# Attention in pairs of tiles: grouping TensorE's whole-array and 64x64 matmuls, with two PSUM tiles for the transposed rows

## The chip, the core and the metric

The kernel runs on one core of a Trainium2 chip. Its time is the device time of one launch in microseconds (us). Before the change the median of three runs is 567.77 us (565.73 to 568.13).

## The reference

An attention over chunks of 64 positions feeds a mixture of experts that picks one expert for each row.

```python
# attention: q, k, v are (8, 8, 576, 64); 9 chunks of 64 for each batch and head
scores = (1 / sqrt(64)) * q_c @ k_c.T            # 64 x 64 for each chunk
attn = exp(scores - max(scores)); attn /= sum(attn) + 1e-9
x = (attn @ v_c), heads side by side             # 4608 rows of 512
# mixture of experts: 8 experts, 512 -> 1024 -> 512
logits = x @ w_gate + modality_bias[modality_id]
e = argmax(logits); gate = softmax(logits)[e]
out = gate * (relu(x @ w1[e]) @ w2[e])
```

## The kernel before

**Attention.** The 4608 rows are 36 tiles of 128 rows (two chunks of 64, all 8 heads). The loop at line 731 takes one tile i at a time, in program order on every engine. For a tile t there are these steps, which run in different turns of the loop:

- scores(t), line 232: TensorE multiplies q by k in 16 pieces of 64x64 into the PSUM tile sp (L239). VectorE takes the row maximum (mx, L241) and subtracts it (ex, L243).
- exps(t), line 246: ScalarE takes exp in place (ex, L248); GpSimd folds the 64 columns to 32 (sr, L249). sums(t), line 251: VectorE sums sr (sm, L253) and takes the reciprocal (ris, L254).
- transposes(t), line 256: four 128x128 transposes of ex on TensorE (ap, L260); ScalarE copies them to SBUF (at, L262).
- values(t), line 265: 16 products of 64x64 with v (xp, L273); ScalarE copies them (xt, L276).
- rows(t), line 279: four whole-array matmuls turn xt back to rows and give the logits (yb, L288). VectorE scales the rows into xr (L290), ScalarE copies the logits (lp, L294) and then issues the write of xr to DRAM (xd, L295).

In turn i TensorE does transposes(i), rows(i-2), scores(i+2) and values(i). The transposes and the rows use the whole array of 128x128; the scores and values work in quarters of 64x64. An fp32 matmul of the program shows as two in the trace, so a step of 16 shows as x32, the rows as x8 and the transposes as x4. [...]

**Loads.** SyncE issues the loads of q and k (load_qk, L113, six buffers) and of v (load_v, L119, five buffers), each when its buffer comes free.

**Routing.** route(g), line 300, works on the logits of a group of tiles. Group 0 has tiles 0 to 13; its steps are the yields of a generator, and advance() takes one more of them after values of each tile (before values it advances only the scatters, as long as fewer than four of those have been issued). In this order the steps are: a product on GpSimd (L309), sums on GpSimd (L314 to L317), the maximum and exp (gmx, L321; ge on ScalarE, L324), one-hot and a prefix sum (oh, scan, L333 and L341), the rest of the prefix sum and a reciprocal, and then two TensorE matmuls (rp, L352 and L353) whose result gives each row its place in a table (pi, L362). 14 scatters by GpSimd (tab, L372) write that table, one for each advance().

**From the table to the first expert.** A table PLAN, by tile number counted from the end of attention, says after which tile SyncE fetches weights (raw, L588) and the row lists (tl, L510), GpSimd gathers the first expert's rows (xg, L531), and ScalarE and VectorE split weights into high and low parts (wh, L599; wl, L603). In the last two turns split(0) and split(1), line 565, transpose the gathered rows (tp, L571) in place of scores; split(2) and split(3) follow. Then come 13 slots of expert work (first, L628, and second, L642), which use yb's three banks as accumulators.

Of the kernel before, what the change touches and what calls it, by code (L numbers as in the profile page):

```python
# [8 lines left out]
F32 = mybir.dt.float32  # L9
# [10 lines left out]
P = 128  # L20
N = B * S
DM = H * D
E = 8
# [68 lines left out]
def attention_moe(ctx: ExitStack, tc: tile.TileContext, qkv, mod, cst, bias, wcat, wfst, out):  # L92
# [17 lines left out]
    def load_qk(t):  # L110
        if t < NT:
            b = wk.tile([P, 2, DM], F32, name="qk", bufs=NB)
            SP.dma_start(b, qkv[t][:, 0:2])  # L113
            st[t] = {"qk": b}
# [46 lines left out]

    yb = ps.tile([P, 3, 512], F32, name="yb", bufs=1)

    def busy(n):
        wps = ps.tile([P, 512], F32, tag="r", name="wps", bufs=1)
        for i in range(n):
            PE.matmul(wps, warm[:, 0:P], warm, start=True, stop=True)

# [110 lines left out]
    def rows(t):  # L279
# [5 lines left out]
        xr = wk.tile([P, NJB, NK, 32], F32, name="xr", bufs=4)  # L285
        fp = yb[:, 0:2, :].rearrange("p b (a c) -> p (b a) c", a=2)
        for p in range(NP):
# [6 lines left out]
        A.copy(lp.rearrange("p (a b) d -> p a (b d)", a=NP), fp[:, :, P:GWC])  # L294
        A.dma_start(xd[t * P:(t + 1) * P, :], xr.rearrange("p j c d -> p (j c d)"))  # L295

# [3 lines left out]
    def route(g):  # L300
# [48 lines left out]
        for _ in range(1 if g < NEG else 5):  # L349
            yield  # L350
        rp = ps.tile([P, 2, 32, E], F32, tag="r", name="rp", bufs=1)
        PE.matmul(rp[:, 0, 0:n], ub, oh, start=True, stop=True)  # L352
# [309 lines left out]
    def slot(s, mid=None):  # L662

        nt = tiles(s)
        end = max(s + 1, NSURE) * NF
        ys = [yb[:, t, :] for t in range(nt)]
        pend = None
# [60 lines left out]
    scores(1)  # L728
    load_qk(NB + 1)
    busy(BUSY)  # L730
    for i in range(NT):
        transposes(i)
        if i + 1 < NT:
            exps(i + 1)
        sums(i)
        load_v(i + NB - 2)
        if i >= 2:
            rows(i - 2)
        if i + 2 < NT:
            scores(i + 2)  # L740
        else:
            split(i + 2 - NT, "s")
        load_qk(i + NB + 2)
        if i >= 6 and i % 3 == 0:
            clear_part()
        advance([pooljobs] if len(marks) < 4 else None)
        values(i)
        advance()
        for g, (a, n) in enumerate(GROUPS):
            if a + n - 1 == i - 2:  # L750
                jobs.append(route(g))
        plan(i - NT)
    rows(NT - 2)
    split(2)
    split(3)
    plan(0)

    def last():
        rows(NT - 1)
        jobs.append(route(len(GROUPS) - 1))  # L760

# [74 lines left out]
```

## Time and profile before

| | |
|---|---|
| median of 3 runs (range) | 567.77 us (565.73 to 568.13) |
| the profiled execution | 568.66 us |
| its span, first to last instruction | 566.8 us |
| its mean granted TensorE clock | 0.996 |
| busy: TensorE, VectorE, ScalarE, GpSimd | 552.4, 362.3, 246.8, 179.7 us |
| chain that ended last: TensorE | 77% |
| attention, from the first transposes to the first expert matmul | 9.6 to 140.2 us |

The span is 1.9 us shorter than the execution's own time, which in turn is 0.9 us above the median of the runs. In rows of the timeline the columns are the start in us, the length in us, the engine, the line, the operation, its output and inputs, the number of instructions merged into the row and, in brackets, how long the engine had been idle before it and what ended that. PE is TensorE's matmuls, DVE is VectorE, ACT ScalarE, POOL GpSimd; a q behind a name is that engine's instruction queue.

### The profile page before, as it was taken

Reading aid. Unit: us, or ns where it says so; the run is one execution under the profiler, and the core shown is the slowest. Engines: PE = TensorE matmul, PEld = TensorE weight load, DVE = VectorE, ACT = ScalarE, POOL = GpSimd, SP = SyncE. Lnnn points to the kernel's source line nnn. Section 1 sums busy time; section 2 is a strip of 40 time slices with the busy share of each in tenths; the row PEclk is TensorE's granted clock in tenths of the full one; section 3 lists DMA queues with packets and bytes.
Section 4 is the critical chain, followed back from the end, with each engine's and each line's share of the span. In section 5 each row is a group of like instructions: output and inputs, shape, how many; then the busy total and the mean of one; then the engine's idle time right before and its main releaser. Section 6 shows DMA issues by size and latency. Waiting matters only on the chain.

```text
span 566.8 us, 12365 instructions
## 1 busy us (share of the span) xinstructions
PE 552.4 (97%) x4900; PEld 499.2 (88%) x4900; DVE 362.3 (64%) x633; ACT 246.8 (44%) x423; POOL 179.7 (32%) x182
## 2 busy tenths in 40 slices
PE   8999999999999999999999999999999999999993
PEld 5899999998889989899898998998898989989992
DVE  4777789867899665655656565565646656556741
ACT  3555555555434344443533434344434343344530
POOL 3312336732658753133230412213041220302101
PEclk9999999999999999999999999999999999999998
DMA  8999998968888647876574866657587673747400
GB/s 305 400 355 371 358 284 288 292 223 333 243 262 239 235 133 253 324 243 211 168 280 144 272 242 181 245 170 256 185 261 245 173 252 112 234 175 242 165 23 26
DMA packets 59538, 133.23 MB, mean 235 GB/s; under 512 B 11022, under 2 KB 29134, under 8 KB 53072
## 3 DMA queue, kind: packets, MB, share of 16 engines
q1 hardware_dynamic: 46784, 101.39, 54.0%
q0 software_dynamic: 7072, 19.18, 10.0%
q10 hardware_dynamic: 5616, 11.80, 5.5%
q8 instruction: 40, 0.66, 0.4%
q14 instruction: 26, 0.21, 0.1%
HBM read 102.16 MB, written 30.70 MB: 234 GB/s over the span
## 4 chain that ended last, share of the span: by engine, by line
PE 77%; issue 13%; POOL 3%; DMA 2%; DVE 2%; ACT 1%; SPq 0%; POOLq 0%; ACTq 0%
PE yb L642 29%; PE hp L628 28%; PE sp L239 6%; PE yb L288 6%; PE xp L273 6%; PE ap L260 3%; POOL out L657 1%; DMA out<-yo,tk 1%; DMA qk<-in_qkv 1%; POOL xg L531 1%; POOL lh L314 0%; DVE wl L603 0%; DVE xr L290 0%; ACT wh L599 0%; POOL lh L315 0%
## 5 line engine op out<-in xcount | busy, mean ns | idle before, releaser
L603 DVE TENSOR_TENSOR wl<-raw,wh 128x1024 fp32r<-128x1024 f32 (+1 forms) x106 | 129.3, 1221 | 35.0 <-ACT wh L599 35.0
L632 ACT ACTIVATE hh<-hp 128x384 fp32r<-128x384 f32 (+1 forms) x104 | 49.3, 474 | 200.6 <-PE hp L628 197.9
L628 PE MATMUL hp<-xl,wh 128*128 128x384 f32 (+1 forms) x416 | 136.4, 328 | 0.1
L628 PE MATMUL hp<-xh,wh 128*128 128x384 f32 (+1 forms) x416 | 136.4, 328 | 0.0
L628 PE MATMUL hp<-xh,wl 128*128 128x384 f32 (+1 forms) x416 | 136.2, 327 | 0.0
L633 DVE SCALAR_TENSOR_TENSOR hl<-hp,hh 128x384 fp32r<-128x384 f32 (+1 forms) x104 | 55.6, 535 | 103.2 <-ACT hh L632 103.2
L642 PE MATMUL yb<-wh,hl 128*128 128x512 f32 x296 | 117.3, 396 | 0.5 <-DVE hl L633 0.5
L642 PE MATMUL yb<-wh,hh 128*128 128x512 f32 x296 | 117.4, 397 | 0.0
L642 PE MATMUL yb<-wl,hh 128*128 128x512 f32 x296 | 116.7, 394 | 0.0
L657 POOL DMA_INDIRECT out<-yo,tk x37 | 47.2, 1275 | 215.8 <-DVE yo L656 187.6
L599 ACT CAST wh<-raw 128x1024 fp32r<-128x1024 f32 (+1 forms) x106 | 108.6, 1025 | 0.2 <-issue 0.2
L628 PEld LDWEIGHTS hp<-xl,wh 128*128 128x128 f32 x416 | 78.2, 188 | 4.2 <-DVE xl L573 0.4
L628 PEld LDWEIGHTS hp<-xh,wh 128*128 128x128 f32 x416 | 78.3, 188 | 4.1 <-ACT xh L572 0.3
L628 PEld LDWEIGHTS hp<-xh,wl 128*128 128x128 f32 x416 | 78.4, 188 | 0.0
L642 PEld LDWEIGHTS yb<-wh,hl 128*128 128x128 f32 x296 | 55.9, 189 | 14.9 <-DVE hl L633 1.4
L642 PEld LDWEIGHTS yb<-wl,hh 128*128 128x128 f32 x296 | 55.7, 188 | 9.6
L642 PEld LDWEIGHTS yb<-wh,hh 128*128 128x128 f32 x296 | 55.6, 188 | 9.0
L531 POOL DMA_INDIRECT xg<-xd,tk x37 | 44.7, 1208 | 21.6 <-issue 12.5
L249 POOL TENSOR_TENSOR sr<-ex 128x256 f32<-128x256 f32 x36 | 26.1, 726 | 68.4 <-ACT ex L248 68.2
L372 POOL DMA_INDIRECT tab<-tg,pi x36 | 39.3, 1092 | 16.7 <-issue 9.4
L239 PEld LDWEIGHTS sp<-qk 64*64 64x64 f32 x1152 | 36.9, 136 | 7.8 <-DMA qk<-in_qkv 2.4
L239 PE MATMUL sp<-qk 64*64 64x64 f32 x1152 | 41.9, 222 | 1.8 <-DMA qk<-in_qkv 1.5
(128 smaller groups left out, 534.2 us busy)
## 6 DMA issues: line engine op xcount, KB each, us to landing
raw<-in_wcat SPq DMA_DIRECT2D x48, 1024.0 KB, 5.8
qk<-in_qkv SPq DMA_DIRECT2D x36, 512.0 KB, 5.3
v<-in_qkv SPq DMA_DIRECT2D x36, 256.0 KB, 6.4
xd<-xr ACTq DMA_DIRECT2D x36, 256.0 KB, 5.8
xs<-xg SPq DMA_DIRECT2D x10, 768.0 KB, 5.7
xq<-xs SPq DMA_DIRECT2D x40, 192.0 KB, 3.5
tab<-raw ACTq DMA_DIRECT2D x3, 768.0 KB, 6.8
raw<-in_wfst SPq DMA_DIRECT2D x4, 512.0 KB, 7.8
```

Of the source, the lines that this page charges most:

```text
L239: PE.matmul(sp[cs_, h, :], b[cs_, 0, hs], b[cs_, 1, hs], start=True, stop=True)
L273: PE.matmul(xp[hs, p, c * 64:c * 64 + 64], v[hs, vs], at[hs, p, c * 64:c * 64 + 64], start=True, stop=True)
L288: PE.matmul(fp[:, p, 0:GWC], xt[:, p, :], gw[:, p, :], start=True, stop=True)
L372: w = G.indirect_dma_start(tab, bass.IndirectOffsetOnAxis(ap=pi[:, j:j + 1], axis=0), tg[:, j, :], None, bounds_check=E * CAP - 1, oob_is_ ...
L531: G.indirect_dma_start(xg[:, t, :], None, xd[0:n, :], bass.IndirectOffsetOnAxis(ap=tk[:, t:t + 1], axis=0), bounds_check=n - 1, oob_is_err ...
L599: A.copy(hi, raw)
L603: (G if pool else V).tensor_tensor(lo, raw, hi.bitcast(F32), ALU.subtract)
L628: PE.matmul(hp, a[:, ks], b[:, k, 0:n], start=(m == 0), stop=(m == 3 * NK - 1))
L632: A.activation(hh[:, 0:n], hp, AF.Relu)
L633: V.scalar_tensor_tensor(hl[:, 0:n], hp, 0.0, hh.bitcast(F32)[:, 0:n], ALU.max, ALU.subtract)
L642: PE.matmul(y, a[:, tsl], b[:, DM:2 * DM], start=(f == 0 and i == 0), stop=(f == NF - 1 and i == 2))
L657: w = G.indirect_dma_start(out, bass.IndirectOffsetOnAxis(ap=tk[:, t:t + 1], axis=0), yo, None, bounds_check=N - 1, oob_is_err=False)
```

## The change

The loop takes two tiles, i and i+1, in one turn. TensorE now does rows(i-2), transposes(i), rows(i-1), transposes(i+1), then scores(i+2), scores(i+3), values(i), values(i+1). In the first turn scores(2) and scores(3) follow the transposes of tile 0 and of tile 1.

- yb becomes two PSUM tiles of two banks each; rows of even tiles use the first, rows of odd tiles the second. The tag "r" is gone: busy writes into the second yb tile, and rp shares the tag "t" with ap and xp. The experts' three accumulators are both banks of the first tile and one of the second.
- The write of xr to DRAM leaves rows() and becomes put(), two of them in ScalarE's queue behind both tiles' copies.
- exps(t+2) stands behind values(t) now, where it stood ahead of scores(t+1); sums(i+1) stands at the end of the turn.
- The loads keep their order by tile; SyncE now gets one v, two qk and one v in each turn.
- The jobs still go forward by one step after values of each tile, and PLAN is still worked off by tile number. split(0) and split(1) both stand ahead of the last two values, with TensorE's transposes of tiles 34 and 35 just before them.

```diff
-    yb = ps.tile([P, 3, 512], F32, name="yb", bufs=1)
+    yb = [ps.tile([P, 2, 512], F32, name=f"yb{i}", bufs=1) for i in range(2)]
 
     def busy(n):
-        wps = ps.tile([P, 512], F32, tag="r", name="wps", bufs=1)
         for i in range(n):
-            PE.matmul(wps, warm[:, 0:P], warm, start=True, stop=True)
+            PE.matmul(yb[1][:, 1], warm[:, 0:P], warm, start=True, stop=True)
...
-        fp = yb[:, 0:2, :].rearrange("p b (a c) -> p (b a) c", a=2)
+        fp = yb[t % 2].rearrange("p b (a c) -> p (b a) c", a=2)
...
-        A.dma_start(xd[t * P:(t + 1) * P, :], xr.rearrange("p j c d -> p (j c d)"))
+        st[t] = xr
+
+    def put(t):
+        A.dma_start(xd[t * P:(t + 1) * P, :], st.pop(t).rearrange("p j c d -> p (j c d)"))
...
-        rp = ps.tile([P, 2, 32, E], F32, tag="r", name="rp", bufs=1)
+        rp = ps.tile([P, 2, 32, E], F32, tag="t", name="rp")
...
-        ys = [yb[:, t, :] for t in range(nt)]
+        ys = [yb[t // 2][:, t % 2] for t in range(nt)]
...
+    exps(1)
     busy(BUSY)
-    for i in range(NT):
-        transposes(i)
-        if i + 1 < NT:
-            exps(i + 1)
+
+    for i in range(0, NT, 2):
+        for t in (i, i + 1):
+            if i:
+                rows(t - 2)
+            transposes(t)
+            if not i:
+                scores(t + 2)
+        load_v(i + NB - 2)
+        if i:
+            put(i - 2)
+            put(i - 1)
         sums(i)
-        load_v(i + NB - 2)
-        if i >= 2:
-            rows(i - 2)
-        if i + 2 < NT:
+        if 0 < i < NT - 2:
             scores(i + 2)
-        else:
-            split(i + 2 - NT, "s")
+            scores(i + 3)
+        elif i:
+            split(0, "s")
+            split(1, "s")
         load_qk(i + NB + 2)
-        if i >= 6 and i % 3 == 0:
+        load_qk(i + NB + 3)
+        if any(t >= 6 and t % 3 == 0 for t in (i, i + 1)):
             clear_part()
         advance([pooljobs] if len(marks) < 4 else None)
-        values(i)
-        advance()
+        for t in (i, i + 1):
+            values(t)
+            if i < NT - 2:
+                exps(t + 2)
+            advance()
+            if t == i:
+                load_v(i + NB - 1)
+                plan(i - NT)
+                advance([pooljobs] if len(marks) < 4 else None)
+        sums(i + 1)
         for g, (a, n) in enumerate(GROUPS):
-            if a + n - 1 == i - 2:
+            if i and a + n - 1 == i - 1:
                 jobs.append(route(g))
-        plan(i - NT)
+        plan(i + 1 - NT)
     rows(NT - 2)
+    put(NT - 2)
```

What this moves can be seen in the engines' instruction lists. TensorE, two tiles in the middle of attention, before (the number behind a name tells buffers apart; x16 are the program's matmuls of one step):

```order
L239 MATMUL sp_1404<-qk_1033 64x64 x16
L273 MATMUL xp_1427<-at_1387,v_1131 64x64 x16
L260 MATMUL ap_1455<-cs_73,ex_1353 128x128 x4
L288 MATMUL yb_103<-cs_73,xt_1374 128x144 x4
L239 MATMUL sp_1477<-qk_1098 64x64 x16
L273 MATMUL xp_1500<-at_1460,v_1195 64x64 x16
L260 MATMUL ap_1524<-cs_73,ex_1423 128x128 x4
L288 MATMUL yb_103<-cs_73,xt_1444 128x144 x4
```

and two tiles now:

```order
L238 MATMUL sp_898<-qk_554 64x64 x16
L238 MATMUL sp_919<-qk_556 64x64 x16
L272 MATMUL xp_944<-at_875,v_633 64x64 x16
L272 MATMUL xp_967<-at_889,v_708 64x64 x16
L287 MATMUL yb0_103<-cs_73,xt_961 128x144 x4
L259 MATMUL ap_998<-cs_73,ex_917 128x128 x4
L287 MATMUL yb1_104<-cs_73,xt_984 128x144 x4
L259 MATMUL ap_1012<-cs_73,ex_938 128x128 x4
```

The steps of 64x64 of both tiles stand together, and so do the whole-array ones: two changes between the kinds in a pair where there were four. Rows of the second tile go to a tile of their own (yb1).

VectorE, from the last steps of group 0's prefix sum (scan) to the first instruction that reads rp (base1), before:

```order
L341 TENSOR_TENSOR scan1_137<-scan0_136 128x112
L341 TENSOR_TENSOR scan0_136<-scan1_137 128x112
L345 TENSOR_REDUCE gs_1590<-ge_1449 128x14
L346 TENSOR_SCALAR gs_1590<-gs_1590 128x14
L348 RECIPROCAL tg0_140<-gs_1590 128x14
L253 TENSOR_REDUCE sm_1603<-sr0_149 128x8
L254 RECIPROCAL ris_148<-sm_1603 128x8
L290 TENSOR_TENSOR xr_1608<-yb_103,ris_148 128x4x4x32
L241 TENSOR_REDUCE mx_1633<-sp_1616 128x8
L243 TENSOR_TENSOR ex_1635<-sp_1616,mx_1633 128x512
L354 TENSOR_TENSOR base1_133<-base0_132,rp_1658 128x8
```

and now, from the scores of the pair on:

```order
L240 TENSOR_REDUCE mx_1577<-sp_1560 128x8
L242 TENSOR_TENSOR ex_1579<-sp_1560,mx_1577 128x512
L240 TENSOR_REDUCE mx_1598<-sp_1581 128x8
L242 TENSOR_TENSOR ex_1600<-sp_1581,mx_1598 128x512
L343 TENSOR_TENSOR scan1_137<-scan0_136 128x112
L343 TENSOR_TENSOR scan0_136<-scan1_137 128x112
L347 TENSOR_REDUCE gs_1629<-ge_1488 128x14
L348 TENSOR_SCALAR gs_1629<-gs_1629 128x14
L350 RECIPROCAL tg0_140<-gs_1629 128x14
L356 TENSOR_TENSOR base1_133<-base0_132,rp_1656 128x8
```

The work of a whole tile that lay between scan and rp is gone from there: both now lie in one pair, behind the scores of both its tiles. On TensorE rp still stands behind the values of tile 21.

GpSimd around the gather of the first expert's rows (tk, xg), before:

```order
L249 TENSOR_TENSOR sr0_149<-ex_2190 128x8x32
L249 TENSOR_TENSOR sr1_150<-ex_2286 128x8x32
L527 COPY tk0_173<-tl0_172 128x3
L531 DMA xg_178<-xd_69,tk0_173 128x512 x3
L249 TENSOR_TENSOR sr2_151<-ex_2350 128x8x32
```

and now:

```order
L248 TENSOR_TENSOR sr0_149<-ex_2204 128x8x32
L248 TENSOR_TENSOR sr1_150<-ex_2225 128x8x32
L248 TENSOR_TENSOR sr2_151<-ex_2364 128x8x32
L529 COPY tk0_173<-tl0_172 128x3
L533 DMA xg_178<-xd_69,tk0_173 128x512 x3
L248 TENSOR_TENSOR sr0_149<-ex_2385 128x8x32
```

sr2 of tile 32 stands ahead of the gather now; the first sum behind the gather is that of tile 33.

More of the change, by code (lines that the diff above doesn't have):

```diff
@@ L759, in last @@
         rows(NT - 1)
+        put(NT - 1)
         jobs.append(route(len(GROUPS) - 1))
```

## The prediction

> **What bounds the kernel now.** I read the busy times by stage first, then the timeline of one tile, then the rows of single lines, and last the waits near the end of attention. Attention and the experts:
>
> ```profile
> 9.60:140.20 130.60, 128.41 (x2678) 120.10 (x2677) 101.38 (x235) 70.55 (x148) 49.21 (x62) 1.00 0.93 325
> ```
>
> The columns are the stretch, its length, the busy time of TensorE, its weight loads, VectorE, ScalarE and GpSimd, the granted clock, the DMA engines' busy share and GB/s. TensorE is busy for 128.4 of attention's 130.6 us. But busy is not full: one tile in the middle shows it.
>
> ```profile
> 72.21 1.03 PE L273 MATMUL xp<-at,v 64*64 64x64 f32 x29
> ...
> 74.80 1.15 PE L239 MATMUL sp<-qk 64*64 64x64 f32 x32
> 75.78 1.10 PE L273 MATMUL xp<-at,v 64*64 64x64 f32 x32
> 76.82 0.65 PE L260 MATMUL ap<-cs,ex 128*128 128x128 f32 x4
> 77.31 1.15 PE L288 MATMUL yb<-cs,xt 128*128 128x144 f32 x8
> 78.38 1.15 PE L239 MATMUL sp<-qk 64*64 64x64 f32 x32
> ```
>
> ```profile
> 69.82 0.49 PE L260 MATMUL ap<-cs,ex 128*128 128x128 f32 x3
> ```
>
> ```profile
> L273 PE MATMUL xp<-at,v x1152: 218/218/267, 11.1 to 138.5; 64*64 64x64 f32 x192
> ```
>
> A tile lasts 78.38 - 74.80 = 3.58 us, and no row in it shows an idle time ahead of it. Now the same matmuls at their own pace. The 29 values last 1.03 us from the first start to the last end; without the last one's 0.218 that is 28 steps in 0.81, 0.029 each, so the 64 of a tile take 1.85. Three transposes last 0.49, one is 0.273 (its median in the line's row), so a step is 0.11 and four take 0.44. The eight rows last 1.15, one is 0.286, a step is 0.123 and eight take 0.98. Together 3.27 us. The remaining 0.31 lies where the kind of matmul changes, twice in a tile: about 0.15 from values to transposes and 0.15 from rows to scores. Rounding in the rows makes it 0.29 to 0.31; I take 0.30. So attention is bound by TensorE's order, and 8% of a tile is the changes.
>
> **The change part by part.** *Changes of kind.* After the first transposes there are now 36 blocks of 64x64 work, one for each tile; with pairs there are 19 (scores(2) alone, then 17 pairs, then the last two values). 17 blocks fewer, each with a way in and a way out: 17 x 0.30 = **5.1 us less**. A pair should take 2 x 3.27 + 0.30 = 6.84 us.
>
> [...]
>
> [...]
>
> *Is a pair still bound by TensorE?* Count from the first scores matmul of a pair: scores to 1.85, values to 3.7, a change, rows at 3.85, transposes at 4.83, rows at 5.27, transposes at 6.25, next scores at 6.84. ScalarE and VectorE in one tile before:
>
> ```profile
> 72.42 0.69 DVE L241 TENSOR_REDUCE mx<-sp 128x8 f32<-128x512 f32 x1 [0.34 <-PE sp L239]
> 73.14 0.69 DVE L243 TENSOR_TENSOR ex<-sp,mx 128x512 f32<-128x512 f32 x1
> ...
> 73.35 0.58 ACT L276 COPY xt<-xp 128x512 f32<-128x512 f32 x1 [1.03 <-PE xp L273]
> ...
> 73.75 0.42 DVE L253 TENSOR_REDUCE sm<-sr 128x8 f32<-128x264 f32 x1
> ...
> 74.20 0.20 DVE L254 RECIPROCAL ris<-sm 128x8 f32<-128x8 f32 x1
> 74.46 0.63 ACT L248 ACTIVATE ex<-ex 128x512 f32<-128x512 f32 x1
> ...
> 74.97 0.69 DVE L290 TENSOR_TENSOR xr<-yb,ris 128x512 f32<-128x512 f32 x1 [0.56 <-DMA v<-in_qkv]
> ```
>
> The scores of this tile start at 74.80 - 3.58 = 71.22; mx follows 1.2 us later, and xt 1.14 us after the values' second matmul (72.21). So the first tile's xt is copied from 3.0 to 3.6, and its rows want it at 3.85: 0.25 to spare, the thinnest cover in the pair. exp of the next tile follows to 4.2 (wanted by the transposes at 4.83), then the second xt to 4.8 (wanted at 5.27) and the second exp to 5.45 (wanted at 6.25). VectorE: 2.69 us a tile, 5.4 of 6.84. Its chain mx, ex, mx, ex runs from 1.2 to 4.0. So a regular pair has no new wait. The two yb tiles let the rows of the second tile run without the evacuation of the first.
>
> *Loads and writes.* Loads of the same bytes come in another grouping; SyncE waits for TensorE to free buffers, not the reverse:
>
> ```profile
> SPq L113 <- PE sp L239: 41.2, 21, 2.3
> ```
>
> ```profile
> xd<-xr ACTq DMA_DIRECT2D x36, 256.0 KB, 5.8
> ```
>
> A q, k load is wanted three pairs, about 20 us, after its issue, and a v load two pairs. The two writes, moved behind both tiles' copies in ScalarE's queue, take 0.33 us each to issue, between 1.1 and 1.8 of the pair, before xt at 3.0. I cost these edits at nothing; if that cover fails, it is rival C.
>
> *Routing.* Two of its steps now wait for a whole pair's scores. The first:
>
> ```profile
> 84.49 0.46 DVE L341 TENSOR_TENSOR scan<-scan 128x112 bf16<-128x112 bf16 x2
> ...
> 87.56 0.22 PE L352 MATMUL rp<-oh,ub 128*128 128x112 bf16 x1
> ```
>
> Before, rp came 2.6 us after the scans and waited for nothing. Now the scans follow the second ex, which starts at 1.2 + 0.72 + 0.62 + 0.72 = 3.26; 0.61 later they start, 0.46 later they end, at 4.35, perhaps 0.3 more because the pair before gives VectorE two steps too. TensorE reaches rp at 3.85. Behind rp stand the rows of the pair and everything after: **0.6 us more**, once (0.3 to 1.0).
>
> ```profile
> 77.93 0.30 ACT L324 ACTIVATE ge<-lg 128x112 f32<-128x112 f32 x1 [0.42 <-DVE lg L322]
> ...
> 113.37 0.62 ACT L599 CAST wh<-raw 128x512 fp32r<-128x512 f32 x1
> ```
>
> The others are on ScalarE. ge, which needs the same late place on VectorE, now stands before a second xt: xt ends near 5.4, wanted at 5.27. The first wh cast (0.62 us) stands before a second xt too, and two xh casts of split before the xt of the last tiles. About 0.15 each, **0.4 us more** (0 to 0.8).
>
> *The gather.* Before, it cost TensorE a wait:
>
> ```profile
> 111.93 0.99 POOL L372 DMA_INDIRECT tab<-tg,pi  x1 [0.16 <-issue]
> ...
> 119.36 3.20 SPq L510 DMA_DIRECT2D tl<-tab  x3
> ...
> 126.11 1.00 POOL L531 DMA_INDIRECT xg<-xd,tk  x1 [0.30 <-issue]
> 127.13 1.41 POOL L249 TENSOR_TENSOR sr<-ex 128x256 f32<-128x256 f32 x2
> 127.59 0.66 PE L260 MATMUL ap<-cs,ex 128*128 128x128 f32 x4
> 127.90 0.43 DVE L253 TENSOR_REDUCE sm<-sr 128x8 f32<-128x264 f32 x1 [3.29 <-POOL sr L249]
> ...
> 129.46 1.25 PE L288 MATMUL yb<-cs,xt 128*128 128x144 f32 x8 [1.22 <-ACT lp L294]
> ```
>
> sr queued behind the gather, sm behind sr, xr and lp behind sm, and the rows behind lp: they start at 129.46 where 127.59 + 0.49 = 128.08 was due, 1.4 us late. Now sr of tile 32 is ahead of the gather, and sr of tile 33, behind it, is read only at the end of the next pair. Its sums run out at about 3.4 of that pair, and sm wants it at 4.0. **1.2 us less** (0 to 1.4).
>
> Sum: -5.1 + 0.6 + 0.4 - 1.2 = -5.3 us. The profiled execution (568.66, span 566.8) would become 563.4 (561.5); it is 0.9 above the median of the runs, so the median goes to 567.77 - 5.3 = **562.5 us**. The experts' order is not changed, and their stage shifts as a whole if its first inputs come in time.
>
> **The rivals.** *A, VectorE becomes the bound while it routes.*
>
> ```profile
> 80.00:110.00 30.00, 30.00 (x634) 28.24 (x631) 28.18 (x88) 16.13 (x34) 18.18 (x22) 1.00 0.93 281
> ```
>
> VectorE (the third busy time) is busy for 28.2 of 30 us there. At 6.84 instead of 7.16 a pair the same work has 28.7. It fits if VectorE hardly idles; if it keeps its 1.8 us of idle, the stretch (4.2 pairs) gains nothing and 4.2 x 0.32 = 1.3 us are lost, with a later rp some 0.7 more: 564.5.
>
> [...]
>
>
> *B, the saved time is waited for at the gathered rows.* From the last scatter's start (111.93) to the third gather's (126.11) are 14.2 us, and the first transposes of gathered rows came at 134. The scatters start only 2.3 us earlier now, because rp stands at the same tile, while those transposes want their rows 4.5 us earlier. I reckon 1 us of slack left; if the chain keeps its old distance and eats 2 us more than that: 565.
>
> *C, slower: ScalarE hands xt over late in every pair.* xt(i) has 0.25 us to spare, and in front of it in ScalarE's queue stand two writes. If their issue blocks until earlier transfers have landed (their median is 5.8 us), xt slips; from 0.25 + 5.3/18 = 0.55 us of slip on all gain is gone. With a slip of 0.9 us in each of 18 pairs the loss is 18 x 0.65 = 11.7: 574. For it: the DMA engines are 93% busy. Against it: the traces show an issue of 0.33 us and no wait on ScalarE for a transfer, and in the program eight issues, more than a pair, lie between two transfers that share a semaphore.
>
> *D, the 0.15 at a change is not the change but a wait for operands*, so merging leaves it there: -1.2 + 1.0, 567.6. Against it: no row of the timeline gives TensorE a releaser there, and the 0.15 is the same before transposes and before scores, whose operands are long ready.
>
> **How the numbers follow.** Forecast as summed, 561.0 to 564.0: 0.60. A 0.14, B 0.13, C 0.06, D 0.07. The range of 8 in 10 runs from 560.9 (no new waits, the gather's wait gone, 0.31 a change) to 566.0 (A and B inside it). About 0.5% (2.8 us) is what a measurement can tell from no change: faster is below 564.9, which the forecast, most of A and a part of B give: 0.75; the same 0.19, from D and the rest of A and B; slower 0.06, C.
>
> **What would show it right or wrong.** Right: from one pair's first scores to the next's 6.84 to 6.87 us, with x64 rows of scores and of values; one idle of about 0.6 us before rp and none of 1.2 us before yb near the gather; the first expert matmul about 5 us earlier than 140.2. Wrong: rows that wait for xt in every pair (C), VectorE without idle and pairs above 7 us from rp on (A), the tp transposes waiting for xg (B), pairs of 7.1 us without a wait (D).

## The result, and the profile after

The changed kernel takes 576.15 us (median of 4 runs, 575.20 to 579.07) against 567.92 us of the kernel before, measured beside it (565.73 to 568.13): a ratio of 1.0156, 95% interval 1.0128 to 1.0185. It is **slower by 1.6%**; I had forecast 562.5, with 566.0 as the upper end. The profiled execution took 575.69 us with a span of 573.9, 7.1 more than before. The first expert matmul comes at 147.37 instead of 140.26, 7.1 us later, so attention holds the whole loss. Ratios and intervals, here and below, leave out executions in a second, slower state and can differ by up to 0.5% from the quotient of the two medians given.

The gain is there. One regular pair of the changed kernel, TensorE's timeline (start, length, engine, line, what):

```profile
70.32 2.08 PE L238 MATMUL sp<-qk 64*64 64x64 f32 x64
72.23 2.03 PE L272 MATMUL xp<-at,v 64*64 64x64 f32 x64
74.20 1.25 PE L287 MATMUL yb<-cs,xt 128*128 128x144 f32 x8
75.28 0.60 PE L259 MATMUL ap<-cs,ex 128*128 128x128 f32 x4
75.72 1.15 PE L287 MATMUL yb<-cs,xt 128*128 128x144 f32 x8
76.70 0.60 PE L259 MATMUL ap<-cs,ex 128*128 128x128 f32 x4
```

The next pair begins at 77.23: 6.91 us instead of 2 x 3.58 = 7.16, with no wait. I had said 6.84. A merged block is worth 0.25 us, not 0.30.

What took it back stands in the waits of TensorE during attention (what waited, for whom: us in total, times, longest; "issue" is idle time for which the profile shows nothing that the engine waited for):

```profile
PE tp L573 <- DMA xg<-xd,tk: 4.0, 2, 2.2
PE xp L272 <- issue: 3.1, 2, 1.7
PE rp L355 <- DVE scan L343: 1.3, 1, 1.3
PE xp L272 <- ACT at L261: 1.3, 1, 1.3
PE sp L238 <- DMA qk<-in_qkv: 0.5, 1, 0.5
PE yb L287 <- ACT xt L275: 0.4, 1, 0.4
```

They sum to 10.6 us. Before they were 2.1: the wait for lp behind the gather, which is gone now, and 0.9 of "issue" in three lines, of which the first is shown:

```profile
PE yb L288 <- ACT lp L294: 1.2, 1, 1.2
PE xp L273 <- issue: 0.4, 1, 0.4
```

The largest of the new waits is at the end, TensorE's timeline from the last transposes on:

```profile
136.28 0.27 PE L573 MATMUL tp<-cs,xg 128*128 128x128 f32 x1
138.80 0.33 PE L573 MATMUL tp<-cs,xg 128*128 128x128 f32 x1 [2.25 <-DMA xg<-xd,tk]
140.90 1.12 PE L573 MATMUL tp<-cs,xg 128*128 128x128 f32 x4 [1.77 <-DMA xg<-xd,tk]
141.95 3.68 PE L272 MATMUL xp<-at,v 64*64 64x64 f32 x64
145.56 1.40 PE L287 MATMUL yb<-cs,xt 128*128 128x144 f32 x8
146.80 0.82 PE L573 MATMUL tp<-cs,xg 128*128 128x128 f32 x6
147.37 0.42 PE L630 MATMUL hp<-xh,wh 128*128 128x384 f32 x1
```

The splits wait for gathered rows, and the values behind them take 3.68 us instead of 2.03. By the busy times by stage (the third number from the end is the granted clock) the clock is halved there:

```profile
130.00:139.00 9.00, 6.75 (x144) 6.38 (x139) 6.15 (x13) 4.64 (x11) 4.33 (x6) 1.00 0.95 335
139.00:146.00 7.00, 5.23 (x71) 4.65 (x71) 2.26 (x5) 1.81 (x4) 0.00 (x0) 0.51 0.62 220
```

The rows are late because the chain that ends in them started later and stretched. GpSimd's timeline, its first and last scatter of the first group and its last gather:

```profile
91.95 1.19 POOL L374 DMA_INDIRECT tab<-tg,pi  x1 [1.21 <-DMA xd<-xr]
...
117.80 0.99 POOL L374 DMA_INDIRECT tab<-tg,pi  x1 [0.30 <-issue]
...
131.11 1.00 POOL L533 DMA_INDIRECT xg<-xd,tk  x1 [0.30 <-issue]
```

Before, these stood at 89.84, 111.93 and 126.11: 2.1, 5.9 and 5.0 us earlier. From its issue the last gather needed 9.7 us to land (the time to landing in the view of its line). Before, the three gathers landed in 7.4 to 7.5 us, so the last one was there by 126.11 + 7.5 = 133.6, half a microsecond ahead of the first split. The first scatter and the first split of the kernel before:

```profile
89.84 1.19 POOL L372 DMA_INDIRECT tab<-tg,pi  x1 [3.20 <-DVE pi L362]
...
134.12 0.49 PE L571 MATMUL tp<-cs,xg 128*128 128x128 f32 x3
```

The stalls for "issue", TensorE's timeline:

```profile
47.67 1.97 PE L272 MATMUL xp<-at,v 64*64 64x64 f32 x61
51.35 0.33 PE L272 MATMUL xp<-at,v 64*64 64x64 f32 x3 [1.71 <-issue]
...
63.65 0.39 PE L272 MATMUL xp<-at,v 64*64 64x64 f32 x6
65.40 1.96 PE L272 MATMUL xp<-at,v 64*64 64x64 f32 x58 [1.36 <-issue]
```

They fall in the middle of a stretch whose operands are all there, and at the same places in other runs: behind the 969th, the 1093rd or the 1218th matmul of the trace. From the first of the two stalls to the second TensorE has 249 matmuls, 249 weight loads and 15 semaphore instructions, 513 together. In the same time two of the packets below end, so I put a packet at 256 instructions, an estimate from these counts. The queue that carries instructions moves packets of 0.67 MB / 41 = 16 KB:

```profile
q8 instruction: 41, 0.67, 0.5%
```

The trace's record of this queue has one packet from 48.93 to 49.86 us, one from 55.27 to 56.21 and one from 63.23 to 64.19. The two stalls (49.63 to 51.35, 64.04 to 65.40) end 1.5 and 1.2 us behind the first and the third. All 24 stalls for "issue" of over 0.8 us between 15 and 75 us, in the profiles of all runs here, end 1.2 to 1.6 us behind the end of such a packet. I read them as TensorE waiting for its next instructions; no run shows that by itself.

And the wait for at, ScalarE's timeline:

```profile
109.17 0.21 ACT L293 COPY lp<-yb 128x64 f32<-128x64 f32 x1 [4.05 <-DVE xr L289]
109.28 0.59 ACT L261 COPY at<-ap 128x512 f32<-128x512 f32 x1
```

with TensorE's values behind it:

```profile
109.92 2.08 PE L272 MATMUL xp<-at,v 64*64 64x64 f32 x64 [1.26 <-ACT at L261]
```

The change calls rows(t - 2) ahead of transposes(t), where the kernel before had it behind. So on ScalarE the copy of lp now stands ahead of the copy of at, lp waits for xr on VectorE, and VectorE had two steps of the early table in front of it.

### The profile page after: what moved, and what is told of

Its sections match the earlier page's. It is cut to its first block, busy times and chain, and to the rows that moved or that the text cites. A ratio compares the mean times of both kernels' runs of the same rounds, so it can differ in the third digit from the quotient of the medians.

```text
span 573.9 us, 12479 instructions
## 1 busy us (share of the span) xinstructions
PE 551.8 (96%) x4900; PEld 500.9 (87%) x4900; DVE 364.0 (63%) x633; ACT 242.7 (42%) x423; POOL 167.8 (29%) x182
## 4 chain that ended last, share of the span: by engine, by line
PE 68%; issue 14%; DMA 6%; POOL 5%; DVE 3%; SPq 1%; ACT 1%; POOLq 0%; ACTq 0%; DVEq 0%
PE yb L644 28%; PE hp L630 28%; PE xp L272 4%; PE yb L287 4%; PE sp L238 3%; POOL tab L374 2%; DMA xg<-xd,tk 2%; PE ap L259 1%; DMA qk<-in_qkv 1%; POOL out L659 1%; DMA tab<-tg,pi 1%; DMA out<-yo,tk 1%; DMA xd<-xr 1%; POOL sr L248 1%; POOL xg L533 0%
## 5 line engine op out<-in xcount | busy, mean ns | idle before, releaser
L659 POOL DMA_INDIRECT out<-yo,tk x37 | 39.0, 1054 | 229.4 <-DVE yo L658 201.2
L533 POOL DMA_INDIRECT xg<-xd,tk x37 | 43.5, 1177 | 30.6 <-PE tp L573 12.6
L287 PE MATMUL yb<-cs,xt 128*128 128x144 f32 x288 | 43.3, 294 | 0.4 <-ACT xt L275 0.4
L272 PE MATMUL xp<-at,v 64*64 64x64 f32 x1152 | 39.3, 224 | 4.3 <-issue 3.1
```

The costliest lines, as they stand in the source:

```text
L272: PE.matmul(xp[hs, p, c * 64:c * 64 + 64], v[hs, vs], at[hs, p, c * 64:c * 64 + 64], start=True, stop=True)
L287: PE.matmul(fp[:, p, 0:GWC], xt[:, p, :], gw[:, p, :], start=True, stop=True)
L533: G.indirect_dma_start(xg[:, t, :], None, xd[0:n, :], bass.IndirectOffsetOnAxis(ap=tk[:, t:t + 1], axis=0), bounds_check=n - 1, oob_is_err ...
L659: w = G.indirect_dma_start(out, bass.IndirectOffsetOnAxis(ap=tk[:, t:t + 1], axis=0), yo, None, bounds_check=N - 1, oob_is_err=False)
```

## The experiments

Theories, named as in the expectations. **G**: the gathered rows come too late for splits that stand ahead of the last values, and the idle time halves the clock. **F**: TensorE's instructions come in fetches of 256 (the estimate above); a pair runs 128 matmuls with 128 weight loads in 3.88 us (70.32 to 74.20), a single tile runs half of that before its whole-array work, 12 matmuls in 1.56 us (76.82 to 78.38 in the profile before); a fetch that is late behind full DMA queues stalls it. **L**: at behind lp. The rivals: **P**, the pairs lose whatever stands beside them; **V**, VectorE is the bound while it routes and repairs only move the wait; **W**, the clock falls for the work's own sake.

The runs were made in five sets, each with the kernel before beside it. In two sets the kernel before took 567 us (567.0, 567.3), as in the first measurement, in three 574 (574.6, 574.2, 573.7). I took them for different chips, and the expectations say so. But the results of the sets of 574.6 and of 567.0, nine minutes apart, carry the same chip number, so it is not known what differs. Ratios are to the kernel before in the same set, and each heading has its time there. The changed kernel itself was run again in the set of 567.0 alone.

### End of attention (kernel before: 574.6 us)

```diff
-            split(0, "s")
-            split(1, "s")
...
-    split(2)
-    split(3)
+    for k in range(NK):
+        split(k, "ts"[k < 2])
```

> The first two splits stand behind the last two tiles' values and rows, as the third and fourth do; nothing else is moved. Theory G (the end of attention: the splits, now ahead of 3.9 us of values, wait for gathered rows that land late, and TensorE, idle by then, loses its clock): the values run from about 136.3 to 140.2 at full clock, the splits behind them wait less than 1 us, the first expert matmul comes at 142 to 143 instead of 147.4, and the time is 570 to 571.5. Theory P (the loss is in the pairs themselves, the wait at the end only takes up what is slack elsewhere): not below 574.5. Theory W (the clock falls for the work's own sake, without an idle time): the values still take 3.7 us, 572.5.

576.53 us, ratio 1.0038 (1.0020 to 1.0057). No wait for gathered rows, clock 1.00, values of 2.08 us, and 1.0 us before the experts, which now wait for the last split's lower half (xl). TensorE's timeline:

```profile
141.40 2.08 PE L272 MATMUL xp<-at,v 64*64 64x64 f32 x64 [0.50 <-ACT at L261]
...
144.49 1.47 PE L573 MATMUL tp<-cs,xg 128*128 128x128 f32 x12
146.97 0.44 PE L630 MATMUL hp<-xh,wh 128*128 128x384 f32 x1 [1.01 <-DVE xl L575]
```

The end behaves as G says, and the clock stays up for the same values, against W. The ratio lies far below 1.0156, but the time is not the one expected, because in this set the pairs from tile 25 to 31 took 8.7 us. These long pairs also gave the last gather, issued at 133.8, 10.7 us until the splits, so this run alone doesn't say that moving the splits removed the wait.

```diff
-    -9: {"fetch": [(1, 1)]},
-    -8: {"locate": [(0,), (1,), (2,)], "hi": [(0, 0)]},
+    -9: {"fetch": [(1, 1), (2, 1)]},
+    -8: {"fetch": [(3, 1)], "locate": [(0,), (1,), (2,)], "hi": [(0, 0)]},
...
-    -1: {"fetch": [(4,)]},
-    0: {"gather": [(1,)], "hi": [(2,)], "lo": [(2,)]},
+    0: {"fetch": [(4,)], "gather": [(1,)], "hi": [(2,)], "lo": [(2,)]},
```

> The two 512 KB weight fetches that were issued beside the gather are issued before the token lists, the 1 MB one after the splits; the gather stays where it is. Theory G with crowding (the gathered rows land 9.7 us after their issue because weights, 2 MB, and loads are moved beside them): landing of the last gather 5 to 7 us, the wait of the two splits 1 to 2 us instead of 4.0, time 571 to 573. Theory G by start (they are late because the scatters start 2.1 us later than before, and end 4.6 later): the wait stays at 3.5 to 4.5 us and the time at 575 to 577. Theory P: no change, 575 to 577.

575.95 us, 1.0026 (1.0006 to 1.0045), no wait for gathered rows, with the splits at their place. But with the same long pairs ahead of the splits the gather had more time, so this alone doesn't say that the fetches were the reason. (The scatters end 5.9 us later than before, not the 4.6 of the expectation.)

```diff
+            wps = ps.tile([P, 512], F32, tag="s", name="wps")
+            for _ in range(18):
+                PE.matmul(wps, warm[:, 0:P], warm, start=True, stop=True)
             split(0, "s")
```

> 18 matmuls of zeros (bf16, 128x512, about 0.21 us each, 3.9 us) stand ahead of the first split, in the time in which TensorE waited for gathered rows. Theory G with the clock: the rows land when they did, the values behind the splits take 2.0 us instead of 3.7 at a granted clock of 1.00, the first expert matmul comes at 145 to 146, the time 573.5 to 574.5. If idle time has no part in the fall of the clock: the values still take 3.7 us, and the time stays at 575.5 to 577.

581.56 us, one run. No wait was left behind the filler, which so only cost its own time: no answer on the clock.

```diff
+        if i == GROUPS[0][1]:
+            jobs.append(route(0))
+            advance([jobs])
...
-        for _ in range(1 if g < NEG else 5):
+        for _ in range(2 if g < NEG else 5):
...
-    -8: {"locate": [(0,), (1,), (2,)], "hi": [(0, 0)]},
+    -8: {"gather": [(0,)], "hi": [(0, 0)]},
```

(locate moved to -10.)

> The first group's routing starts one pair earlier, so that rp comes one pair (6.9 us) earlier and one step later behind its scans, and the token lists and the gather of the first slot are asked for one pair earlier. The order of TensorE is otherwise the same. Theory G: rp no longer waits (1.3 us), the scatters start near 84, the splits find their rows (4.0 us) and the clock stays (1.7 us): the first expert matmul near 140.5, time 568 to 570. Theory V (VectorE is the bound while it routes, so the wait only moves to another line): 1 to 2.5 us of waits for at or xt beside the routing stay, time 570 to 572. Theory P: not below 574.

577.80 us, 1.0061 (1.0035 to 1.0087). No wait for scan or gathered rows, but VectorE, in order, waited 5.25 us for GpSimd's sums of lg, xr and lp behind it, and at behind lp: 3.4 us of waits for at, with the clock halved for 3.4 us behind the longer one (2.21). V in part: the same lateness came out at another line.

### The changed kernel again, and its parts (567.0 us)

> The changed kernel once more, unaltered, so that the others of this call have it on the same chip: the first chip's ratio to the kernel before was 1.016; on a second chip, on which the kernel before took 574.6 us, the variants so far had ratios of 1.003 to 1.006. If the loss belongs to the kernel: 1.012 to 1.018 here too. If it was mostly the chip: 1.003 to 1.006.

577.42 us, 1.0191 (1.0174 to 1.0208): the loss belongs to the kernel, at least where the kernel before takes 567 us.

> The kernel before, unaltered, for its profile on the same chip. Theory F (TensorE's instructions come in fetches of 256, and where a fetch is late TensorE stalls; the old order has 128 instructions of 64x64 work in a row, the new one 256): stalls of at most 1 us in sum at those places, a tile of 3.58 us, against 2 to 4 us in the changed kernel. If the chip is the cause: as many as in the changed kernel.

One run, 571.19 us, above the 566.4 to 567.7 of the others. No stall for "issue" at all, and 7.16 us (once 7.23) for every two tiles up to 127 us; then TensorE's timeline has

```profile
130.27 2.08 PE L288 MATMUL yb<-cs,xt 128*128 128x144 f32 x8 [2.35 <-ACT lp L294]
```

and the busy times by stage right behind it

```profile
130.50:133.90 3.40, 3.40 (x38) 3.12 (x39) 2.57 (x6) 1.74 (x4) 0.73 (x1) 0.50 1.04 380
```

So the kernel before has the same fragility: behind a wait of 2.35 us at the gather the clock is 0.50 for 3.4 us. Behind the 1.22 us of its first profile (rows from 129.46 on) it stays at 1.00.

```diff
-        A.copy(lp.rearrange("p (a b) d -> p a (b d)", a=NP), fp[:, :, P:GWC])
-        st[t] = xr
+        st[t] = xr, lp, fp
...
     def put(t):
+        xr, lp, fp = st.pop(t)
+        A.copy(lp.rearrange("p (a b) d -> p a (b d)", a=NP), fp[:, :, P:GWC])
```

> On ScalarE the two copies of lp, which wait for xr on VectorE, stand behind the two copies of at instead of ahead of them; in the kernel before at stood ahead too. Theory L (the change put at behind lp, so that VectorE's lateness while it routes reaches TensorE through at): the 1.2 us of wait for at near 109 goes, the wait for scan stays at 1.3, the time falls by 1 to 2 us against the changed kernel on the same chip. Theory V (VectorE is late for everything, and the wait moves to xt or yb): less than 0.5 us.

576.47 us, 1.0167 (1.0150 to 1.0184): the wait for at is gone (L), but the time is only 1.0 less than the changed kernel's. Where the rest went is the clearest reading of the study. TensorE's timeline of the changed kernel in this set, last transposes and first expert matmul:

```profile
139.85 0.60 PE L259 MATMUL ap<-cs,ex 128*128 128x128 f32 x4
...
148.72 0.42 PE L630 MATMUL hp<-xh,wh 128*128 128x384 f32 x1
```

and with lp behind at:

```profile
136.81 0.60 PE L259 MATMUL ap<-cs,ex 128*128 128x128 f32 x4
...
140.42 0.47 PE L574 MATMUL tp<-cs,xg 128*128 128x128 f32 x1 [2.58 <-DMA xg<-xd,tk]
142.47 1.11 PE L574 MATMUL tp<-cs,xg 128*128 128x128 f32 x4 [1.58 <-DMA xg<-xd,tk]
143.52 3.49 PE L272 MATMUL xp<-at,v 64*64 64x64 f32 x64
...
148.60 0.42 PE L631 MATMUL hp<-xh,wh 128*128 128x384 f32 x1
```

3.0 us earlier at the last tile, 0.1 at the experts. (Of the 3.0, 2.6 lie in one pair, in which the changed kernel's weight cast on ScalarE, ahead of xt, waited 2.86 us for its fetch, against 1.19 here and 0.63 in the first profile. So most of the 3.0 is not the edit's own.) The time saved is waited for at the gathered rows, at 4.2 us instead of 2.0.

The next has both edits above and this:

```diff
+            if t == GROUPS[0][1] + 1:
+                jobs.append(route(0))
             advance()
...
-        for _ in range(1 if g < NEG else 5):
+        for _ in range(2 if g < NEG else 5):
```

> Three edits at once: the splits behind the last values, lp behind at, and the first group's routing begun half a pair earlier with rp at its old place. Theory G with L: the waits for gathered rows (4.0 us), for scan (1.3), for at and xt (1.6) and the lower clock (1.7) go, the instruction stalls (2 to 4) stay: 7 to 9 us less than the changed kernel, within 1.5 us of the kernel before. If pairs are worth what I forecast and instruction stalls are the chip's: 2 to 4 us faster than the kernel before. Theory P: at most 3 us less than the changed kernel.

572.23 us, 1.0104 (1.0066 to 1.0142): 5.2 less than the changed kernel in the same set, no wait for scan or gathered rows, clock 1.00, the first expert matmul at 145.00 instead of 148.72. Less than expected: 3.5 us of instruction stalls are left and 4.7 of waits for xt, at and ex, 1.8 of them behind a weight cast, the others beside the routing (VectorE waits 3.84 us for lg).

### Instructions, half the pairs, and one term alone (567.3 us)

```diff
-            SP.dma_start(b, qkv[t][:, 2])
-            st[t]["v"] = b
+            if t < NB - 1:
+                vs.append(wk.tile([P, DM], F32, name="v", bufs=NB - 1))
+                SP.dma_start(vs[t], qkv[t][:, 2])
+            st[t]["v"] = vs[t % (NB - 1)]
```

> The changed kernel without the loads of v for tiles 5 to 35 (31 x 256 KB, a quarter of attention's reads); their values are computed from the v of the first five tiles, so that work is left out of the transfers alone. Theory F (a late fetch of TensorE's instructions, held up by full DMA queues): the stalls inside the 64x64 stretches (1.5 to 3.1 us in the changed kernel's runs) fall below 0.5 us, all pairs before rp last 6.9 us, and the last tile comes 2 to 4 us earlier. If the stalls are TensorE's own: they stay at 1.5 us or more. The time: theory G has the gathered rows wait take back half of it or more, 1 to 3 us less than the changed kernel; if nothing waits there, 3 to 5.

570.50 us, 1.0061 (1.0040 to 1.0081). From 10 to 70 us the DMA engines' share is 0.86 instead of 1.00, and of TensorE's waits

```profile
PE tp L576 <- DMA xg<-xd,tk: 2.2, 2, 1.6
PE rp L358 <- DVE scan L346: 1.3, 1, 1.3
PE xp L275 <- ACT at L264: 1.3, 1, 1.3
PE xp L275 <- issue: 0.6, 1, 0.6
```

the stalls are 0.6 instead of 1.5 and 3.1; the waits of L and G, which have nothing to do with it, stay. F: with transfers taken away the same order of instructions stalls little, in the one profile taken; all other profiles with pairs have 1.3 us or more of such stalls between 20 and 75 us.

```diff
+PAIRS = 18
...
-    for i in range(0, NT, 2):
+    for i in range(0, PAIRS, 2):
...
+    for i in range(PAIRS, NT):
+        transposes(i)
...
+        rows(i - 2)
+        put(i - 2)
```

(From tile 18 on the old loop, with rows in the even PSUM tile only, and rp in the odd one's second bank.)

> Pairs for tiles 0 to 17 only; from tile 18, ahead of the routing's work on VectorE, the order of the kernel before, one tile at a time with one pair of banks for the rows. Eight blocks of 64x64 work are merged instead of 17. Theory G and V (the loss comes from what the pairs meet behind tile 18: routing, weight casts, gather, splits): ratio to the kernel before 0.996 to 1.002, that is 8 x 0.25 = 2.0 us gained less 1 to 3 us of instruction stalls. Theory P (pairs as such lose): half of the loss stays, ratio 1.006 to 1.010.

573.08 us, 1.0121 (1.0086 to 1.0157), against G and V, and above the range of P too. The profile (571.38 us, the shortest of six executions up to 578.18) has the first expert matmul at 140.79, 0.5 later than before, with

```profile
PE xp L273 <- issue: 2.7, 3, 1.6
PE xp L273 <- ACT at L262: 1.1, 1, 1.1
PE sp L239 <- DMA qk<-in_qkv: 0.8, 1, 0.8
```

so even the half without routing gains nothing: 2.0 us of merged blocks less 2.7 of stalls. The remaining 2.2 us are my edit's own: rp shares an accumulator's PSUM tile, and a matmul of the experts waits 2.22 us for it, at 164.33. The run cannot tell G from P by its time.

```diff
+        if t == 32:
+            return
         G.tensor_tensor(sring[t % 3][:, :, 0:32], ex[:, :, 0:32], ex[:, :, 32:64], ALU.add)
...
-        V.reduce_sum(sm, sring[t % 3], axis=AX.X)
+        V.reduce_sum(sm, st[t]["ex"] if t == 32 else sring[t % 3], axis=AX.X)
+        if t == 32:
+            V.tensor_scalar_add(sm, sm, 1e-9)
```

> As the run with pairs up to tile 17, and the sums of tile 32 are made by VectorE from ex itself, not behind the gather on GpSimd (128x512 instead of 128x264 elements, 0.3 us more, and one small addition). The wait of the rows behind lp near the gather (1.2 and 2.4 us in the two profiles of the kernel before) goes: 1.0 to 2.4 us less than with the pairs alone, ratio to the kernel before 0.993 to 0.999, unless the splits wait for the gathered rows in its place: then less than 0.5 us.

574.88 us, 1.0130 (1.0107 to 1.0153): the wait for lp is gone, and the splits wait 4.3 us for gathered rows in its place, in the profile of 580.43 us, the longest of the six executions.

> The kernel before with the sums of tile 32 made by VectorE alone, nothing else: the part of the forecast that the wait behind the gather can go and is worth 1.2 us. 1.0 to 2.4 us less than the kernel before, ratio 0.996 to 0.998; if the splits then wait for the gathered rows, 0.999 to 1.001.

570.93 us, 1.0045 (1.0018 to 1.0072): a little slower, which neither expectation has. The profiled run (566.60 us) has what the forecast's term promised, the first expert matmul at 138.42, 1.8 us earlier, though the splits now wait a little:

```profile
132.44 0.33 PE L575 MATMUL tp<-cs,xg 128*128 128x128 f32 x1 [0.68 <-DMA xg<-xd,tk]
```

But the 12 runs are of two kinds: five from 565.8 to 568.2 us with a mean clock of 0.992 to 0.996, seven from 570.8 to 572.8 at 0.988 to 0.992. I read the second kind as longer waits at that line with the clock halved behind them; no profile fell on one, so this is argued.

### Repairs (574.2 us)

```diff
             transposes(t)
+            if t == GROUPS[0][1] + 8:
+                advance([jobs])
...
+        if i in (22, 24):
+            advance([pooljobs])
...
-    -8: {"locate": [(0,), (1,), (2,)], "hi": [(0, 0)]},
-    -7: {"lo": [(0, 0)], "hi": [(0, 1)]},
-    -6: {"gather": [(0,)], "lo": [(0, 1)]},
+    -7: {"gather": [(0,)], "hi": [(0, 0)]},
```

(locate at -9, the other casts at odd steps, lp behind at as above.)

> The changed kernel in pairs to the end, with four repairs: rp stands behind the next pair's first transposes; lp behind at; one more scatter in each of two pairs, so that the token lists are asked for half a pair earlier and the gather too; each weight cast stands behind both xt of its pair. Theory G with L and F (the loss is waits that the pairs made late, their doubled price by the halved clock, and instruction stalls): no wait for scan, gathered rows or raw, no fall of the clock, 1.5 to 3.5 us of instruction stalls left: ratio to the kernel before 0.994 to 0.999. Theory P (pairs lose whatever stands beside them): 1.006 or more. Theory V (VectorE is the bound while it routes): waits for at and xt of 2 us or more, 1.000 to 1.005.

581.00 us, 1.0112 (1.0065 to 1.0158). The waits for scan, at, xt and the weights are gone, 1.2 us for gathered rows is left, but 6.0 us of stalls for "issue", and the clock is halved behind one of 1.84 us, and once more, from 103.7 us on for 6.8, beside several of 0.4:

```profile
52.50:55.90 3.40, 3.40 (x17) 3.39 (x16) 0.69 (x1) 1.37 (x3) 0.73 (x1) 0.50 1.01 401
```

The next is the same with `bufs=4` for q and k, and their loads four tiles ahead.

> The repaired pairs with four buffers for q and k instead of six: 1 MB less to catch up with, so that the DMA engines are full for a shorter time. Theory F: the DMA share falls below 0.9 ahead of 50 us and the stalls inside the 64x64 stretches to 0 to 1 us: 1 to 2.5 us less than the run with the four repairs alone, ratio 0.990 to 0.996. Against it: waits for qk of 1 us or more in several pairs, then slower than that run.

584.30 us, 1.0157 (1.0108 to 1.0206): not faster, with stalls of 7.9 us. But the DMA engines, at 0.84 from 20 to 30 us, are full again from 40 to 50 (1.03), so the edit did not give F the condition that it asks for.

> The kernel with the 18 matmuls of zeros ahead of the first split once more, on another chip: on the one it ran on, the pairs lasted 8.7 us behind tile 25 and nothing waited for gathered rows, so it told nothing of the clock. If an idle time of 2 us or more halves the clock for the next 3.4 or 6.8 us (the traces with such an idle time have it, those without have not): clock 1.00 up to the end, values of 2.0 us behind the splits, 1.5 to 3 us less than the changed kernel's ratio of 1.016 to 1.019, so 1.011 to 1.015. If not: 1.016 to 1.020.

584.86 us, 1.0141 (1.0088 to 1.0194). Clock 1.00 through attention and values of 2.08 us, but again nothing had to wait behind the filler. The ratio lies in the range expected, but not for the reason given there, and the run does not show that an idle time is what halves the clock.

> The kernel with the weight fetches moved away from the gather once more, on another chip, for the same reason. Gather slowed by the fetches beside it: the last gather lands within 6 us of its issue instead of 7.8 to 10.3, the splits wait less than 1.5 us, the clock stays, ratio 1.004 to 1.010. Late by its start alone: landing 7.5 us or more, waits of 2 us or more, ratio 1.014 to 1.020.

582.38 us, 1.0091 (1.0056 to 1.0125). The last gather, issued at 135.52, is waited for until 142.77: 7.2 us, less than the 7.8 to 10.3 of pairs with the fetches beside it, more than the 6 expected. Since the kernel before lands its gathers in 7.4 to 7.5 us with the same fetches beside them, a part of crowding in the landing is not shown.

### Once more (573.7 us)

> The pairs with the four repairs once more, on whatever chip comes: on the one they ran on, the kernel before took 574.2 us, not 567, and TensorE stalled in the stretch of the scatters, four or five matmuls at a time, which the profiles on the first chips do not show. Theory G with F: if such stalls belong to that chip, the ratio here is 0.996 to 1.004, with 2 to 4 us of instruction stalls and no wait above 1.3 us beside them. If the pairs lose for a reason that no theory has: 1.008 or more without waits to account for it.

576.95 us, 1.0065 (1.0043 to 1.0087), in such a set again and between the two expectations. No wait above 0.54 us beside 6.6 of "issue", and the clock stays at 1.00. While the scatters run, TensorE's timeline is

```profile
101.53 0.33 PE L269 MATMUL xp<-at,v 64*64 64x64 f32 x4 [0.42 <-issue]
...
103.00 0.39 PE L269 MATMUL xp<-at,v 64*64 64x64 f32 x6 [0.41 <-issue]
```

The last run has both edits to the kernel before: the sums of tile 32 on VectorE and the moved fetches.

> The kernel before with the sums of tile 32 on VectorE and the weight fetches moved away from the gather. The sums alone had given runs of two kinds, 566 to 568 us at a mean clock of 0.994 to 0.996 and 570 to 573 at 0.988 to 0.992. Theory G (the lower kind are runs in which the splits waited for gathered rows and the clock halved; rows that land earlier make them rare): all runs of the first kind, ratio 0.996 to 0.999. If the landing does not depend on the fetches: both kinds again, ratio 1.003 to 1.006.

574.35 us, 1.0004 (0.9990 to 1.0018): neither expectation. Its profile shows that in this set the old order too loses in the scatters, 8.66 us for two tiles instead of 7.16 (transposes at 100.06 and 108.72); the pairs take 9.9 there.

## Why the prediction was wrong

**The changes of kind**: right in kind, a sixth too large. 17 x 0.25 = 4.2 us, not 5.1. Rival D is out, and C too: no pair waits for xt as a rule.

**The gather's wait, -1.2**: it went, as predicted, and in the old order alone its going brought 1.8 us in the one profile, where the rows landed nearly in time (138.42 against 140.26). But it was not removed; it had hidden the next one.

**The step that failed** is rival B's reckoning: "the scatters start only 2.3 us earlier now, because rp stands at the same tile [...] I reckon 1 us of slack left; if the chain keeps its old distance and eats 2 us more than that: 565." They start 2.1 us later, end 5.9 later, and the last gather is issued 5.0 later and lands 2.2 slower, while both splits now stand ahead of the last two tiles' values. There was half a microsecond of slack, not enough for any of it. B's place was right, but I had put it at 2.5 us (565 against 562.5) with a chance of 0.13; it cost 4.0 us and, on top, 1.65 for the halved clock, which I had not priced at all. The two variants that kept 4 us of wait at the splits (lp behind at, 1.0167; half the pairs with the sums of tile 32 on VectorE, 1.0130) stayed near the loss.

**Routing**: rp waited 1.3, not 0.6: the steps of VectorE that I counted at their free durations took longer (va 0.69 instead of 0.28 us, with GpSimd's sr beside it from 81.49 to 82.32). I let only rp and ge wait; I followed at through TensorE's count but not through ScalarE's queue, where the change had put lp, and so VectorE, in front of it: 1.3 us. That is near rival A's amount (1.3 and 0.7), by another road. The weight cast ahead of xt, which I priced at 0.15, cost 0.4 us in the first profile and 2.6 in the second (the set of 567.0), because the cast itself waited for its fetch.

**"I cost these edits at nothing"**: the loads did cost nothing by their bytes. What I had put at nothing is TensorE's own instructions: the merged stretch runs 256 of them in 3.9 us without whole-array work between, and attention has 3.1 us of such stalls in the first profile and 1.7 in the second, where the old order has 0.9 and none. Slower had a chance of 0.06, all of it from C: that the other rivals and the terms put at nothing could together take more than the gain was not in the sum.

The ledger of the profiled runs: -4.2 and -1.2 (lp), then +1.3 (rp), +1.3 (at), +0.4 (xt), +0.5 (first q and k), +2.2 (stalls), +4.0 (gathered rows), +1.65 (clock) give +5.9. The rest of the 7.1 is, as an estimate, some 0.5 us for the four transposes at half the clock (140.90 to 141.95) and, for the other part, that a wait is counted from the modelled end of the matmul before it: the pairs with stalls of 1.71 and 1.36 last 8.89 and 8.59 us (second transposes at 45.22 and 54.11, 61.20 and 69.79), 1.98 and 1.68 more than 6.91.

Shown: the wait for gathered rows takes back what is saved ahead of it (lp behind at); with the splits behind the values it and the half clock are gone, in both runs that have the splits there; at waits because of lp; the stalls in the 64x64 stretches end 1.2 to 1.6 us behind an instruction packet, and in one profile without most v loads they are 0.6 us. Read from the traces, not from a run that removes it: that idle time halves the clock (the last section has the figures). Argued: that TensorE waits there for the packet's instructions, and that full DMA queues make the packets late. Open: what, beside the waits for at and xt, stretches the changed kernel's scatters from 22.1 to 25.9 us, and why its gathers take 0.3 to 2.2 us longer to land; what makes the sets of 574 us differ; whether the repaired pairs would win where the kernel before takes 567. No version here beats the kernel before.

## What to carry to other kernels

Count the slack of each transfer chain at the point where its result is used before speeding up what stands ahead of it: here half a microsecond decided over 5. When calls are reordered for one engine, write out the queue of every other engine that they issue to; lp ahead of at was two lines in the diff. And price a wait on TensorE beyond its length: behind waits of 2.35 us (the kernel before) and of 2.25 and 1.77 us (the changed one) the clock was 0.50 for 3.4 and 6.8 us, and in the changed kernel the values alone took 1.65 us more.

## What the hardware did that I had not expected

The clock falls to 0.50 for 3.4 us, or twice that, in the middle of busy work. In each trace all its falls stand on one grid of 3.413 us: in the second profile of the changed kernel they begin at 123.50, 143.97 and, at the end, 570.64 us, 6 and 125 steps apart (447.14 us in 131 steps), in the first at 139.08 and, at the end, 569.16, 126 steps apart (430.08 us). What goes with the falls is the idle time inside one step of that grid, by the busy times by stage:

| profile | step, us | TensorE busy, of 3.41 us | clock in the next step |
|---|---|---|---|
| changed kernel, first | 135.67 to 139.08 | 1.16 | 0.50 |
| changed kernel, second | 120.09 to 123.50 | 0.78 | 0.50 |
| half the pairs | 159.70 to 163.11 | 2.26 | 1.00 |
| half the pairs | 163.11 to 166.53 | 2.20 | 1.00 |
| half the pairs, sums of tile 32 on VectorE | 168.53 to 171.94 | 1.18 | 0.50 |

The last three rows are one and the same wait for rp, 2.2 us: it falls into two steps in one run and into one step in the other. The 1.90 us stall of the run with three edits (49.59 to 51.49) is cut by a step's end too, at 50.94, and leaves the clock alone. Over all profiles, between 9 and 250 us, TensorE was idle for 1.7 us or more in 14 steps, and 13 of them have the half clock behind them (not 134.39 to 137.81 of the last run in the table, with 1.99 us); no fall follows a step with less than 1.28 us; between these it goes both ways.

At steps of about 256 instructions TensorE stalls for up to 1.9 us (three edits); the old order, with DMA shares just as high as the changed kernel's (1.00 from 10 to 70 us in both), stalled 0.6 in that stretch. And the same kernel took 567 or 574 us in different sets; in the second kind short stalls, some 0.4 us after every four to six matmuls, fill the stretch in which the scatters run.
